# Top-k attention and an MLP mixer: the first five pairs without the adding DMA, another start, orders refitted

## The chip, the cores and the metric

The kernel runs on one core of one Trainium2 chip. The metric is device microseconds (us) of one execution; the time before is a median of 760.9 us over three runs (759.42 to 762.38). A core has a matrix engine (PE, fed by weight loads, PEld), a vector engine (DVE), a scalar engine (ACT), a general engine (POOL), a queue engine that issues transfers (SP), and 16 DMA engines. Each engine works through its own instructions strictly in the order in which they were written down, so a wait of one instruction holds all that stand behind it on that engine.

## The reference

Inputs are q, k and v of 8 batches, 8 heads, 576 rows and 64 columns, in 32 bits, and four weights of a mixer.

```
scores = scale * q @ k^T                      # per batch and head, 576 x 576
kth    = the 32nd largest of each row
scores = where(scores >= kth, scores, -1e9)
attn   = softmax(scores) ; y = attn @ v
x      = y, heads side by side                # per batch 576 x 512
h      = relu(x^T @ w_tok1) @ w_tok2 ; u = x + h^T
out    = u + relu(u @ w_ch1) @ w_ch2
```

## The kernel before

*Pairs, groups and frames.* Two heads make a pair; there are 32 pairs, four to a batch. Of a pair's 2 × 576 score rows the kernel makes five groups (g = 0 to 4): four with 128 rows of each head, and one with the last 64 rows of both. So a pair has nine frames of 128 rows, and the whole work 288.

*The way of a group.* q and k are loaded (L393, L401, L408), turned on PE (`turn`, L426), and kept as qT and kT in SBUF by ACT (L430, L433). PE multiplies them (L488, or L494 for g = 4) into PSUM, ACT copies the scores into a tile Sb (L578). DVE takes the eight largest of each seventh of a row (L588, seven to a row) and from these 56 finds a first threshold in five steps (L593 to L600). POOL negates it (ng, L609) and turns the row's scores into integers that rise above it (L632); ACT counts with Sign how many do (L635); POOL puts eight dummy values, chosen by the count, behind the row (L638); and a last DVE maximum over 584 values (tlo, L643) gives the exact 32nd largest. POOL then makes from it (nt, L651) a mask U, in which what isn't wanted is very low (L666).

*The two ways to the weights.* For most groups (`low` in the code) PE adds the mask in PSUM (L510, L500) and multiplies qT and kT once more on top (L488, L504), and ACT takes the Exp of that into a tile Pm (L676; L682 for g = 4). For the groups listed in `ADDED` ACT takes the Exp straight from Sb, early (L625), into a tile Pe, and POOL issues a DMA that adds the mask U to it in SBUF (L686). In both ways SP then issues a transposing DMA into PT (L690), PE multiplies PT with v (L706), and DVE divides (L715, L716). There are two Pm tiles and four Pe tiles; a tile is free again when its transpose has landed. Before the change one group of every pair but the last is in `ADDED` (g = 1), and in pairs 22 to 30 a second.

*The mixer* of a batch follows its four pairs and is spread over the next ones; its weights come by DMAs that POOL issues at set times in the first 130 us (L336, L346). They are not counted as transfers by the planner.

*The order.* Nothing is ordered by hand. `Plan.add` takes each piece of work with its engine, a planned duration, a due time, what it depends on, and which buffers it takes; `Plan.run` lays them out one after the other: on each engine the piece that can start first, and among those within a few hundredths of a us the one with the least due time. A due time is T × (number of the frame) plus a number for the kind of work from the table `DUE`. So T, `DUE` and the planned durations set the order of all instructions, and nothing else does; real times come out otherwise. `Plan.between` afterwards puts dummy matmuls (`filler`, L368 and L370) into the longer free times that PE has in the plan between 15 and 140 us, to keep its clock up.

*The start.* The first pair has pieces of its own (L446 to L477): k's two heads are issued by ACT and SP; then SP issues the first quarter of q's rows (`some_q(0, 1)`, two transfers), the rest (two) and the last 64 rows (`tail_q`, two, L460), and ACT the last rows of k (L467). PE turns k's first three blocks (k0), q's first quarter (o0), k's last two (k1), and q's other four (o1). Before all this stand the constants: POOL makes an identity (identF), DVE copies it as identB and identN (L313, L314), and then zeroes the last blocks of the q and k tiles (L318), which the loads of those rows have to wait for.

Of the kernel before, what the change touches and what calls it, by code (L numbers as in the profile page):

```python
# [26 lines left out]
ADDED = {(p, 1) for p in range(31)} | {(p, 3) for p in range(22, 31)}  # L27
# [184 lines left out]
def kernel(  # L212
# [98 lines left out]

    make_identity(nc, identF[:, :])
# [4 lines left out]
    for t in qLs + kLs:  # L317
        nc.vector.memset(t[:, 4, :, :], 0.0)  # L318
# [43 lines left out]

    def filler(s, k):
        a = 1024 * s + 1024 - 184

        def f():
            if k is not None:
                nc.tensor.matmul(out=bank[:, a : a + 1], lhsT=identF[:, :], rhs=thi[:, k : k + 1], start=True, stop=True)  # L368
            for _ in range(6):
                nc.tensor.matmul(out=bank[:, a : a + 184], lhsT=identB[:, :], rhs=identF[:, :].bitcast(bf16)[:, 0:184],  # L370
                                 start=True, stop=True)

        return f
# [10 lines left out]
    def pair_ops(p):  # L384
# [51 lines left out]
        if p > 0:  # L436
# [6 lines left out]
            eq = [plan.add("ACT", 0.62, tc_, lambda: keep_q(0, PW), [oq], use=[pq, qT])] * 2  # L443
            ek = [plan.add("ACT", 0.54, tc_ + 0.5 * T, lambda: keep_k(nc.scalar.copy, 0, S), [ok], use=[pk, kT])] * 2
        else:
            def some_q(lo, hi):  # L446
                def f():
                    for h in range(2):
                        nc.sync.dma_start(
                            out=qL.t[:, lo:hi, h, :],  # L450
                            in_=q[b, h0 + h, 0:SM, :].rearrange("(p t) d -> p t d", t=4)[:, lo:hi, :])
                return f
# [24 lines left out]
            eq.append(plan.add("ACT", 0.55, -96.0, lambda: keep_q(P, PW), [o1], use=[pq, qT]))  # L477
# [91 lines left out]
        for g in range(5):  # L569
# [36 lines left out]
        for gs in JOINED if p < END else ((0, 1), (2,), (3,), (4,)):  # L606
            lo, hi = at(frame(gs[-1])[1] + frame(gs[-1])[0] - 1), at(frame(gs[0])[1]) + 1
            nb = Buf("ng")
            o = plan.add("POOL", 0.285, frame(gs[-1])[2] + DUE["ng"], lambda lo=lo, hi=hi, nb=nb: nc.gpsimd.tensor_scalar(  # L609
                out=nb.t[:, 0 : hi - lo], in0=thi[:, lo:hi], scalar1=-1.0, scalar2=None, op0=ALU.mult),  # L610
                         sum((cand[g] for g in gs), []), acq=[nb])
            for g in gs:
                neg[g] = (o, nb, lo)
        for g in range(5):
# [10 lines left out]
            oe = [] if low else [plan.add("ACT", 1.2 if n == 2 else 0.67, t + DUE["ex1"], lambda n=n, Sb=Sb, Pm=Pm: nc.scalar.activation(  # L625
# [4 lines left out]
            for h in range(n):  # L630
# [7 lines left out]
            dm = plan.add("POOL", 0.27, t + DUE["dum"], lambda n=n, i0=i0, X=X: nc.gpsimd.tensor_tensor(  # L638
# [10 lines left out]
        for gs in SETS if p < END else [(g,) for g in range(5) if g not in DIRECT]:  # L649
            nt, lo, hi = Buf("nt"), at(frame(gs[-1])[1] + frame(gs[-1])[0] - 1), at(frame(gs[0])[1]) + 1  # L650
            o = plan.add("POOL", 0.29, frame(gs[-1])[2] + DUE["nt"], lambda lo=lo, hi=hi, nt=nt: nc.gpsimd.tensor_scalar(  # L651
# [4 lines left out]
        for g in range(5):  # L656
# [13 lines left out]
            if low and n == 2:  # L670
                oe = []
                for i in range(2):
                    orr = plan.add("PE", 0.486 if i else 1.18, t + DUE["re"] + 0.01 * i, lambda g=g, i=i, s2=s2, U=U: (
# [11 lines left out]
            else:  # L685
                oe = [plan.add("POOL", 1.08, t + DUE["u"] + 0.02, lambda n=n, U=U, Pm=Pm: nc.gpsimd.dma_start(  # L686
# [45 lines left out]
    def mlp_ops(b):  # L732
# [34 lines left out]
        for cc in range(NC):  # L767
# [23 lines left out]
            ut.append(plan.add("ACT", 0.54, due(0.0) + 1, lambda cc=cc, pb=pb: nc.scalar.copy(  # L791
# [6 lines left out]
        for fc in range(NF):  # L798
# [19 lines left out]
        for s0 in (0, 2, 4) if odd else (0, 2):  # L818
# [4 lines left out]
            for sc in range(s0, s0 + w):  # L823
                for part in range(2):
# [14 lines left out]
                    d = due(1.57 if part else 1.3)  # L839
                    o = plan.add("PE", 1.57 if part else 1.3, d, f, (h2 + wl["c2"] + more) if o is None else [o],  # L840
# [293 lines left out]
    hints = {next(i for i, o in enumerate(order) if o.start > plan.span - d): e for e, d in HINTS.items()}  # L1134
    for i, o in enumerate(order):
# [193 lines left out]
```

## Time and profile before

| | |
|---|---|
| median of three runs | 760.9 us (759.42 to 762.38) |
| the profiled execution | 763.86 us, span 762.1 us |
| busy: PE, DVE, ACT, POOL | 728.7, 718.8, 684.4, 586.4 us |
| DMA | 101.15 MB, 133 GB/s in the mean |

The profile is of one execution, with times from its span's start. The views that the prediction shows are: the busy time of each engine in stretches of the span (with the number of instructions in brackets, the granted clock of PE, and the share of the DMA engines that was busy); the instructions in order of time, with what ended an engine's idle time before one of them in square brackets; the waits, as total, number and longest; the chain of work that ended last, followed back from the end; and groups of like instructions, with their number, busy time and mean duration in ns. A name like "Pm<-bank" is what an instruction writes and reads, L676 a line of the kernel. Matmuls are pipelined and their ends are modelled, so neighbours overlap. A small q behind an engine's name means its queue: an instruction that only issues or waits.

### The profile page before, as it was taken

The page shows a single profiled execution, that of the slowest core. Times are in us where ns is not written, and L with a number is a line of the kernel's source. Part 1 is how long each engine was busy: PE and PEld are TensorE (multiplying, and loading weights), DVE is VectorE, ACT ScalarE, POOL GpSimd, SP SyncE. Part 2 cuts the span into 40 slices and gives each one's busy share as a digit, 9 for nine tenths or more (in the row PEclk, how much of TensorE's full clock was granted, in tenths as well). Part 3 has the DMA queues.
Part 4 walks back from the last instruction along what each step waited for, and adds up shares of the span by engine and source line. Part 5 has one row for each costly group of instructions (what it writes and reads, how often), then busy time and mean ns, then how long its engine had stood idle before and what let it go on. Part 6 is the DMA issues. An engine that isn't in the chain of part 4 may idle for free.

```text
span 762.1 us, 21660 instructions
## 1 busy us (share of the span) xinstructions
PE 728.7 (96%) x6517; PEld 508.1 (67%) x6517; DVE 718.8 (94%) x4466; ACT 684.4 (90%) x1350; POOL 586.4 (77%) x1053
## 2 busy tenths in 40 slices
PE   6989999999999999999999999999989999999997
PEld 4766777677657776667666765667747776677663
DVE  7997999999999999999999999999999999999861
ACT  5868999899889998999989998899989999999852
POOL 3696989987877878778787878877789888988600
PEclk9998999999999999999999999999999999999999
DMA  5598999967887678767787656887759988876602
GB/s 124 91 157 145 142 158 180 170 124 118 148 147 140 125 115 163 151 119 128 118 157 151 121 108 123 168 162 126 139 115 166 152 135 160 137 125 88 123 18 72
DMA packets 293658, 101.15 MB, mean 133 GB/s; under 512 B 269856, under 2 KB 290208, under 8 KB 293536
## 3 DMA queue, kind: packets, MB, share of 16 engines
q1 hardware_dynamic: 279152, 83.86, 59.0%
q0 software_dynamic: 13632, 15.57, 14.6%
q8 instruction: 52, 0.85, 0.4%
q14 instruction: 70, 0.57, 0.2%
q10 hardware_dynamic: 752, 0.30, 0.1%
HBM read 35.85 MB, written 9.44 MB: 59 GB/s over the span
## 4 chain that ended last, share of the span: by engine, by line
DVE 41%; PE 39%; ACT 8%; POOL 6%; issue 3%; DMA 2%; ACTq 0%; DVEq 0%; POOLq 0%; SPq 0%
DVE cd L588 16%; PE bank L488 13%; DVE tlo L643 12%; PE bank L830 4%; PE bank L805 4%; PE bank L706 3%; ACT sign L635 3%; DVE cd L598 3%; PE bank L510 2%; DVE cd L594 2%; POOL U L666 2%; DVE Xb L716 2%; DVE thi L600 2%; PE bank L494 2%; POOL Sb L632 2%
## 5 line engine op out<-in xcount | busy, mean ns | idle before, releaser
L588 DVE MAX8 cd<-Sb 128x8 f32<-128x82 f32 (+1 forms) x2016 | 386.3, 231 | 2.0 <-ACT Sb L578 1.9
L488 PE MATMUL bank<-kT,qT 64*128 64x288 f32 x1712 | 242.2, 422 | 6.2 <-ACT kT L433 3.8
L635 ACT ACTIVATE sign<-Sb,half 128x576 bf16<-128x576 int32 x283 | 226.9, 802 | 20.4 <-POOL Sb L632 12.9
L666 POOL TENSOR_SCALAR U<-Sb,nt 128x576 uint8<-128x576 int32 x283 | 212.3, 750 | 25.7
L632 POOL TENSOR_SCALAR Sb<-Sb,ng 128x576 int32<-128x576 f32 x283 | 217.2, 779 | 13.2 <-ACT Pe L625 6.0
L643 DVE MAX8 tlo<-Sb 128x8 f32<-128x584 uint32 x283 | 214.0, 756 | 8.8 <-POOL Sb L638 8.0
L488 PEld LDWEIGHTS bank<-kT,qT 64*128 64x128 f32 x1712 | 153.9, 188 | 72.7 <-issue 21.7
L578 ACT COPY Sb<-bank 128x576 f32<-128x576 f32 x288 | 167.5, 685 | 10.3 <-PE bank L488 7.5
L676 ACT ACTIVATE Pm<-bank 128x576 bf16<-128x576 f32 x172 | 105.4, 664 | 7.3 <-PE bank L488 7.1
L805 PE MATMUL bank<-UT,wc1b 128*128 128x288 bf16 x672 | 90.2, 286 | 3.6 <-ACT UT L791 1.5
L830 PE MATMUL bank<-wc2b,H 128*128 128x512 bf16 x372 | 88.1, 379 | 0.4 <-ACT H L811 0.4
L805 PEld LDWEIGHTS <-wc1b 128*128 128x128 bf16 x672 | 64.6, 98 | 27.1 <-issue 9.3
L830 PEld LDWEIGHTS <-H 128*128 128x128 bf16 x372 | 34.6, 98 | 40.8 <-issue 6.0
L635 ACT ACTIVATION_READ_ACCUMULATOR sign<-Sb,half 128x1 f32 x283 | 61.7, 218 | 0.0
L651 POOL TENSOR_SCALAR nt<-tlo 128x2 f32<-128x2 f32 (+1 forms) x157 | 35.8, 228 | 32.3 <-DVE tlo L643 12.8
L510 PE MATMUL bank<-U,identN 128*128 128x288 bf16 x344 | 58.1, 288 | 1.2 <-POOL U L666 0.5
L600 DVE MAX8 thi<-cd 128x8 f32<-128x56 f32 x288 | 58.3, 202 | 0.0
L686 POOL DMA_DIRECT2D Pe<-U x40 | 50.4, 1259 | 6.7 <-POOL U L666 4.5
L811 ACT ACTIVATE H<-bank 128x576 bf16<-128x576 f32 x84 | 54.4, 676 | 0.0
L638 POOL TENSOR_TENSOR Sb<-kdum,cnt 128x16 int32<-128x16 int32 (+1 forms) x157 | 36.7, 235 | 21.5 <-ACT sign L635 17.7
L598 DVE MATCH_REPLACE8 cd<-m,cd 128x35 f32<-128x35 f32 x288 | 52.5, 182 | 0.0
L596 DVE MAX8 m<-cd 128x8 f32<-128x35 f32 x288 | 51.9, 180 | 0.1
(140 smaller groups left out, 1067.9 us busy)
## 6 DMA issues: line engine op xcount, KB each, us to landing
Pe<-U POOLq DMA_DIRECT2D x40, 288.0 KB, 4.7
vL<-in_v_dram SPq DMA_DIRECT2D x32, 256.0 KB, 3.0
kL<-in_k_dram SPq DMA_DIRECT2D x63, 128.0 KB, 3.1
qL<-in_q_dram SPq DMA_DIRECT2D x62, 128.0 KB, 2.9
out_dram<-ob SPq DMA_DIRECT2D x15, 512.0 KB, 3.0
wc1b<-in_moe_w_ch_dram POOLq DMA_DIRECT2D x4, 384.0 KB, 5.1
wc2b<-in_moe_w_ch_dram POOLq DMA_DIRECT2D x4, 384.0 KB, 6.5
PT<-Pm SPq DMA_TRANSPOSE x86, 3.9
```

The costliest lines, as they stand in the source:

```text
L488: nc.tensor.matmul(out=halves(s.t)[:, h, :], lhsT=qT.t[rows(h), g * P : (g + 1) * P], rhs=kT.t[rows(h), i * HS : (i + 1) * HS], start=star ...
L578: ev.append(plan.add("ACT", 0.535, t + DUE["cp"] + 0.01 * i, lambda n=n, i=i, s1=s1, Sb=Sb: nc.scalar.copy(out=Sb.t[:, 0:n, i * HS : (i + ...
L588: ss.append(plan.add("DVE", 0.146, t + DUE["seg"] + 1.0 * h, lambda a=a, h=h, cd=cd, Sb=Sb: nc.vector.max(cd.t[:, a, :], Sb.t[:, h, bounds ...
L598: a4 = plan.add("DVE", 0.157, tr_, lambda m8=m8, cd=cd: nc.vector.match_replace(cd.t[:, :, 0:5], m8.t[:, 1, :], cd.t[:, :, 0:5], NEG), [a3 ...
L600: a5 = plan.add("DVE", 0.12, tr_, lambda i=i, cd=cd: nc.vector.max(thi[:, at(i) - 7 : at(i) + 1], cd.t[:, :, :]), [a4] + tops[-1:], use=[cd])
L632: xo.append(plan.add("POOL", 0.725, t + DUE["x"] + 0.9 * h, lambda k=at(i) - lo, h=h, Sb=Sb, X=X, nb=nb: nc.gpsimd.tensor_scalar(out=X.t[: ...
L635: sgn.append(plan.add("ACT", 0.77, t + DUE["sg"] + 0.8 * h, lambda i=i, h=h, X=X: nc.scalar.activation(out=sign[:, :], in_=X.t[:, h, 0:S]. ...
L643: mxs.append(plan.add("DVE", 0.67, t + DUE["mx"] + 1.2 * h, lambda i=i, h=h, X=X: nc.vector.max(tlo[:, at(i) - 7 : at(i) + 1], X.t[:, h, : ...
L666: us.append(plan.add("POOL", 0.84, t + DUE["u"] + 0.01 * h, lambda h=h, k=at(i0 + h) - lo, nt=nt, U=U, X=X: nc.gpsimd.tensor_scalar(out=by ...
L676: oe.append(plan.add("ACT", 0.54, t + DUE["ex"], lambda i=i, s2=s2, Pm=Pm: nc.scalar.activation(out=Pm.t[:, :, i * HS : (i + 1) * HS], in_ ...
L805: nc.tensor.matmul(out=o[:, i, :], lhsT=wc1b[:, cc, fc * P : (fc + 1) * P], rhs=UT.t[:, cc, i * HS : (i + 1) * HS], start=(cc == 0), stop= ...
L830: nc.tensor.matmul(out=po, lhsT=H2.t[:, fc, cs], rhs=wc2b[:, fc, :], start=(fc == 0), stop=False)
```

## The change

1. `ADDED` loses g = 1 of pairs 0 to 4: these five groups go the way of most groups, over Pm.
2. The memsets of the last blocks of the q and k tiles (L318) are moved ahead of the identity.
3. In the first pair q's first quarter is loaded with one transfer for both heads in place of two, and q's last 64 rows are turned and kept by pieces of their own (o2 and a third entry of eq), so that the products of g = 1 to 3 wait for o1 alone.
4. Thirteen dummy matmuls (`warm(3, 13)`) go to the head of PE's work, and three more behind the turning of q's first quarter; the planner counts k's first loads as one us each in place of a half.
5. T, all of `DUE` and some ten planned durations have other values.

```
-ADDED = {(p, 1) for p in range(31)} | {(p, 3) for p in range(22, 31)}
+ADDED = {(p, 1) for p in range(5, 31)} | {(p, 3) for p in range(22, 31)}
...
-T = 1.71610
+T = 1.64060
...
+    for t in qLs + kLs:
+        nc.vector.memset(t[:, 4, :, :], 0.0)
     make_identity(nc, identF[:, :])
...
-    for t in qLs + kLs:
-        nc.vector.memset(t[:, 4, :, :], 0.0)
...
+    def warm(s, n):
+        a = 1024 * s + 1024 - 184
+        for _ in range(n):
+            nc.tensor.matmul(out=bank[:, a : a + 184], lhsT=identB[:, :], rhs=identF[:, :].bitcast(bf16)[:, 0:184],
+                             start=True, stop=True)
...
+            def first_q():
+                nc.sync.dma_start(
+                    out=qL.t[:, 0, :, :],
+                    in_=q[b, h0 : h0 + 2, 0:SM, :].rearrange("h (p t) d -> p t h d", t=4)[:, 0, :, :])
+
+            def more_q():
+                for h in range(2):
+                    nc.sync.dma_start(
+                        out=qL.t[:, 1:4, h, :],
+                        in_=q[b, h0 + h, 0:SM, :].rearrange("(p t) d -> p t d", t=4)[:, 1:4, :])
...
-            la = plan.add("ACT", 0.7, -99.0, main_k(0, nc.scalar), acq=[kL], dma=0.5)
-            lb = plan.add("SP", 0.7, -99.0, main_k(1, nc.sync), [], use=[kL], dma=0.5)
-            q0 = plan.add("SP", 1.3, -98.0, some_q(0, 1), acq=[qL], dma=0.2)
-            q1 = plan.add("SP", 1.3, -97.0, some_q(1, 4), use=[qL], dma=0.7)
+            la = plan.add("ACT", 0.7, -99.0, main_k(0, nc.scalar), acq=[kL], dma=1.0)
+            lb = plan.add("SP", 0.7, -99.0, main_k(1, nc.sync), [], use=[kL], dma=1.0)
+            q0 = plan.add("SP", 0.7, -98.0, first_q, acq=[qL], dma=0.2)
+            q1 = plan.add("SP", 1.3, -97.0, more_q, use=[qL], dma=0.7)
...
-            o0 = plan.add("PE", 0.22, -98.0, turn(pq, qL, (0,)), [q0], acq=[pq, qT], use=[qL])
+            def turn_first():
+                turn(pq, qL, (0,))()
+                warm(3, 3)
+
+            o0 = plan.add("PE", 0.7, -98.0, turn_first, [q0], acq=[pq, qT], use=[qL], lat=-0.3)
             k1 = plan.add("PE", 0.43, -97.0, turn(pk, kL, (3, 4)), [k0, lc], use=[pk, kT, kL])
-            o1 = plan.add("PE", 0.86, -96.0, turn(pq, qL, (1, 2, 3, 4)), [o0, q1, q2], use=[pq, qT, qL])
+            o1 = plan.add("PE", 0.65, -97.5, turn(pq, qL, (1, 2, 3)), [o0, q1], use=[pq, qT, qL])
+            o2 = plan.add("PE", 0.22, -96.0, turn(pq, qL, (4,)), [o1, q2], use=[pq, qT, qL])
...
-            eq.append(plan.add("ACT", 0.55, -96.0, lambda: keep_q(P, PW), [o1], use=[pq, qT]))
+            eq.append(plan.add("ACT", 0.45, -96.5, lambda: keep_q(P, SM), [o1], use=[pq, qT]))
+            eq.append(plan.add("ACT", 0.25, -96.0, lambda: keep_q(SM, PW), [o2], use=[pq, qT]))
...
-                    [eq[g > 0]] + ek[: i + 1 if n == 2 else 2], acq=[s1[i]] + ([Sb] if i == 0 else []), use=[qT, kT, Sb], mode=3 if n == 2 else 0)
+                    [eq[0 if g == 0 else 1 if g < 4 else 2]] + ek[: i + 1 if n == 2 else 2], acq=[s1[i]] + ([Sb] if i == 0 else []), use=[qT, kT, Sb], mode=3 if n == 2 else 0)
...
     hints = {next(i for i, o in enumerate(order) if o.start > plan.span - d): e for e, d in HINTS.items()}
+    warm(3, 13)
     for i, o in enumerate(order):
```

More of the change, by code (lines that the diff above doesn't have):

```diff
@@ L361 @@
             moe_w_ch2[3 * i * P : (3 * i + 3) * P, :].rearrange("(j p) c -> p j c", p=P)))
+    def warm(s, n):
[3 more added lines that the diff above has]
+                             start=True, stop=True)
     def filler(s, k):
-        a = 1024 * s + 1024 - 184
         def f():
             if k is not None:
+                a = 1024 * s + 1024 - 184
                 nc.tensor.matmul(out=bank[:, a : a + 1], lhsT=identF[:, :], rhs=thi[:, k : k + 1], start=True, stop=True)
-            for _ in range(6):
-                nc.tensor.matmul(out=bank[:, a : a + 184], lhsT=identB[:, :], rhs=identF[:, :].bitcast(bf16)[:, 0:184],
-                                 start=True, stop=True)
+            warm(s, 6)
         return f
@@ L442, in pair_ops @@
             tc_ = t0 + DUE["ck"]
-            eq = [plan.add("ACT", 0.62, tc_, lambda: keep_q(0, PW), [oq], use=[pq, qT])] * 2
+            eq = [plan.add("ACT", 0.62, tc_, lambda: keep_q(0, PW), [oq], use=[pq, qT])] * 3
             ek = [plan.add("ACT", 0.54, tc_ + 0.5 * T, lambda: keep_k(nc.scalar.copy, 0, S), [ok], use=[pk, kT])] * 2
         else:
[L446 to L452, printed above, removed]
+            def first_q():
[7 more added lines that the diff above has]
+                        in_=q[b, h0 + h, 0:SM, :].rearrange("(p t) d -> p t d", t=4)[:, 1:4, :])
             def main_k(h, eng):
@@ L608, in pair_ops @@
             nb = Buf("ng")
-            o = plan.add("POOL", 0.285, frame(gs[-1])[2] + DUE["ng"], lambda lo=lo, hi=hi, nb=nb: nc.gpsimd.tensor_scalar(
+            o = plan.add("POOL", 0.23, frame(gs[-1])[2] + DUE["ng"], lambda lo=lo, hi=hi, nb=nb: nc.gpsimd.tensor_scalar(
                 out=nb.t[:, 0 : hi - lo], in0=thi[:, lo:hi], scalar1=-1.0, scalar2=None, op0=ALU.mult),
@@ L634, in pair_ops @@
                     op0=ALU.add, op1=ALU.mult), [no] + oe, use=[Sb, nb]))
-                sgn.append(plan.add("ACT", 0.77, t + DUE["sg"] + 0.8 * h, lambda i=i, h=h, X=X: nc.scalar.activation(
+                sgn.append(plan.add("ACT", 0.72, t + DUE["sg"] + 0.8 * h, lambda i=i, h=h, X=X: nc.scalar.activation(
                     out=sign[:, :], in_=X.t[:, h, 0:S].bitcast(i32), func=AF.Sign, bias=half[:, :],
                     accum_out=cnt[:, i : i + 1]), [xo[h]], use=[X], lat=0.7))
-            dm = plan.add("POOL", 0.27, t + DUE["dum"], lambda n=n, i0=i0, X=X: nc.gpsimd.tensor_tensor(
+            dm = plan.add("POOL", 0.22, t + DUE["dum"], lambda n=n, i0=i0, X=X: nc.gpsimd.tensor_tensor(
                 out=X.t[:, 0:n, S:XW].bitcast(i32), in0=kdum[:, :].unsqueeze(1).to_broadcast([P, n, NDUM]),
@@ L685, in pair_ops @@
             else:
-                oe = [plan.add("POOL", 1.08, t + DUE["u"] + 0.02, lambda n=n, U=U, Pm=Pm: nc.gpsimd.dma_start(
+                oe = [plan.add("POOL", 0.95, t + DUE["u"] + 0.02, lambda n=n, U=U, Pm=Pm: nc.gpsimd.dma_start(
                     out=Pm.t[:, 0:n, 0:S].bitcast(u16), in_=U.t[:, 0:n, :], accum_op=ALU.add), us, use=[U, Pm], lat=4.1, dma=1.02 * n)]
@@ L790, in mlp_ops @@
             o = plan.add("PE", 0.98, due(0.98), f, [h1] + wl["w2"], acq=[pb] + ([UT] if cc == 0 else []), use=[X, H1, pb])
-            ut.append(plan.add("ACT", 0.54, due(0.0) + 1, lambda cc=cc, pb=pb: nc.scalar.copy(
+            ut.append(plan.add("ACT", 0.58, due(0.0) + 1, lambda cc=cc, pb=pb: nc.scalar.copy(
                 out=UT.t[:, cc, 0:S].rearrange("p (a b) -> p a b", a=2), in_=halves(pb.t)), [o],
@@ L838, in mlp_ops @@
                     more = ([tails["h2"]] + ut[NC:]) if s0 == 4 else []
-                    d = due(1.57 if part else 1.3)
-                    o = plan.add("PE", 1.57 if part else 1.3, d, f, (h2 + wl["c2"] + more) if o is None else [o],
+                    d = due(1.57 if part else 1.14)
+                    o = plan.add("PE", 1.57 if part else 1.14, d, f, (h2 + wl["c2"] + more) if o is None else [o],
                                  acq=[pb, ob] if o is None else [], use=[pb, H2] + ([UT] if part else []))
```

18 lines of the change are left out of this document (9 added, 9 removed).

## Prediction, made before the changed kernel was run

> **What bounds the kernel now.** I read the busy times first, then the stretches: where each engine is busy, and where the vector engine (DVE) is not.
>
> ```profile
> PE 728.7 (96%) x6517; PEld 508.1 (67%) x6517; DVE 718.8 (94%) x4466; ACT 684.4 (90%) x1350; POOL 586.4 (77%) x1053
> ```
>
> ```profile
> core 0: us, PE busy (x) PEld busy (x) DVE busy (x) ACT busy (x) POOL busy (x), PEclk, DMA share, GB/s
> 9.00:60.00 51.00, 43.53 (x368) 33.87 (x369) 50.66 (x365) 37.07 (x72) 33.93 (x63) 0.98 0.77 125
> 60.00:70.00 10.00, 10.00 (x98) 6.70 (x98) 4.89 (x27) 8.03 (x17) 5.35 (x9) 0.77 0.91 139
> 70.00:712.00 642.00, 627.30 (x5630) 436.94 (x5628) 633.94 (x3990) 612.26 (x1215) 535.73 (x966) 1.00 0.78 138
> 712.00:762.00 50.00, 43.40 (x413) 28.13 (x410) 24.90 (x59) 24.71 (x44) 7.08 (x8) 0.99 0.31 74
> ```
>
> From 9 to 712 us DVE is busy for 689.5 of 703 us, and the change gives it no less to do. So only four things can be won: a start before 9 us, the 5.1 us idle at 60 to 70, the 8.1 us spread over 70 to 712, and something of the last 50 us, which are a chain through PE. The hole at 60 to 70 is the only large one; the waits and the order of time of that stretch follow it back.
>
> ```profile
> DVE tlo L643 <- POOL Sb L638: 4.6, 1, 4.6
> PE bank L368 <- ACT qT L430: 3.9, 1, 3.9
> ACT Pm L682 <- DMA PT<-Pm: 2.7, 1, 2.7
> ```
>
> ```profile
> 40.73 1.27 POOL L686 DMA_DIRECT2D Pe<-U  x1
> ...
> 45.50 1.19 ACT L676 ACTIVATE Pm<-bank 128x576 bf16<-128x576 f32 x2 [2.01 <-PE bank L488]
> ...
> 47.27 1.35 SPq L690 DMA_TRANSPOSE PT<-Pe  x1
> ...
> 48.72 2.68 SPq L690 DMA_TRANSPOSE PT<-Pm  x1
> ...
> 48.84 0.77 POOL L346 DMA_DIRECT2D ob<-in_moe_w_tok_dram  x1
> ...
> 56.78 0.65 ACT L682 ACTIVATE Pm<-bank 128x576 bf16<-128x576 f32 x1 [2.65 <-DMA PT<-Pm]
> ...
> 59.53 4.21 PE L488 MATMUL bank<-kT,qT 64*128 64x288 f32 x16
> 63.68 1.10 PE L510 MATMUL bank<-U,identN 128*128 128x288 bf16 x4
> 64.71 2.21 PE L488 MATMUL bank<-kT,qT 64*128 64x288 f32 x16
> ...
> 66.49 0.77 DVE L643 MAX8 tlo<-Sb 128x8 f32<-128x584 uint32 x1 [4.62 <-POOL Sb L638]
> ...
> 68.66 0.22 DVE L715 RECIPROCAL rds<-bank 128x10 f32<-128x10 f32 x1 [0.45 <-PE bank L706]
> ```
>
> ```profile
> 48.72 7.98 DMA PT<-Pm
> ```
>
> Read it backwards. DVE stood 4.62 and 0.45 us (5.07 in all). PE behind it had first stood 3.9 us, then run cold: the same sixteen products took 4.21 us and, once the clock was back, 2.21. PE stood because ACT stood 2.65 us, in order, at L682, which needs one of the two Pm slots; that slot was still being read by the transpose issued at 48.72, which took 7.98 us to land. That Pm had been ready at 46.69 (45.50 + 1.19). It was issued 2.03 us later because SP issues in order and ahead of it stood the transpose of Pe, which waits for the adding DMA of 40.73 to land. I call all this the hold.
>
> **The first five pairs without the adding DMA.** Five groups of pairs 0 to 4 go the way the others go.
>
> ```profile
> L488 PE MATMUL bank<-kT,qT 64*128 64x288 f32 x312 | 46.4, 435 | 1.9 <-ACT kT L433 1.4 <-ACT Sb L578 0.5
> L370 PE MATMUL bank<-identF,identB 128*128 128x184 bf16 x324 | 30.4, 244 | 1.7 <-ACT Pm L676 0.9 <-ACT kT L433 0.7
> L676 ACT ACTIVATE Pm<-bank 128x576 bf16<-128x576 f32 x30 | 18.4, 654 | 2.1 <-PE bank L488 2.0
> L510 PE MATMUL bank<-U,identN 128*128 128x288 bf16 x60 | 10.9, 295 | 0.9 <-POOL U L666 0.5 <-ACT Pm L682 0.3
> L625 ACT ACTIVATE Pe<-Sb 128x1152 bf16<-128x1152 f32 x7 | 8.2, 1173 | 0.0
> L686 POOL DMA_DIRECT2D Pe<-U x5 | 6.3, 1265 | 0.9 <-POOL U L666 0.6 <-POOL nt L651 0.2
> ```
>
> These groups are the stretch from 15 to 140 us. POOL loses 5 × 1.265 = 6.3 us and the DMA engines five transfers of 288 KB. ACT swaps one 1.17 us Exp for a pair of evictions (1.19 us by the x2 row above): nothing. PE gains per group 4 of L510 (10.9/60 × 4 = 0.73) and 8 of L488 (46.4/312 × 8 = 1.19), together 1.92, so 9.6 us over five. This is hidden by the dummy matmuls of L370, 30.4 us in the same stretch, which the planner puts only into free time of PE; without that cover it would cost the 9.6 us, since PE is the neighbour that fills Sb.
>
> What it does to the hold: no transpose waits for an adding DMA any more, so the transposes behind it go out up to 2.03 us earlier and the slot is free by as much. Of ACT's 2.65 us 0.6 stay. PE then stands some 1.9 instead of 3.9 us and, I assume, keeps its clock: L488 falls by 2.00 (4.21 - 2.21), and L510's first four by about 0.4 (1.10 against 4 × 0.18). 2.03 + 2.00 + 0.4 = 4.4 of 5.07. Bounds: nothing (the transpose at 48.72 met the weight load issued at 48.84, and that stays) and all 5.07. I take -4.4, as the wait in the Pm row starts with the late issue. POOL's 1.26 us, gone from each of four more pairs, meets 8.06 us of DVE idle over 70 to 712; I take -0.5 for it, bounds 0 and -1.5.
>
> The Trainium skill, page "DMA: Bandwidth & Descriptors", section "Issuing engines are not separate DMA queues", says that transfers of all issuing engines run on the same 16 DMA engines and interleave. By that rule the whole 7.98 us is crowding, the late issue is worth little, and the hold term would lie nearer to 0 than to -4.4; the landing of 7.98 us right beside the weight load agrees with it.
>
> **The start.**
>
> ```profile
> 1.33 1.51 DVE L313 CAST identB<-identF 128x128 bf16<-128x128 f32 x1 [1.33 <-POOL identF masks.py:199]
> ...
> 1.48 2.32 SPq L449 DMA_DIRECT2D qL<-in_q_dram  x4
> ...
> 2.88 0.30 DVE L318 MEMSET qL<- 128x128 f32 x2
> ...
> 3.36 0.65 ACTq L467 DMA_DIRECT2D kL<-in_k_dram  x1
> ...
> 3.85 0.87 PE L426 MATMUL bank<-identF,kL 128*128 128x128 f32 x3 [3.85 <-DMA kL<-in_k_dram]
> ...
> 6.18 0.47 PE L426 MATMUL bank<-identF,kL 128*128 128x128 f32 x1 [0.33 <-DMA kL<-in_k_dram]
> ...
> 7.96 0.64 ACT L578 COPY Sb<-bank 128x576 f32<-128x576 f32 x1 [2.35 <-PE bank L488]
> ...
> 8.63 0.68 DVE L588 MAX8 cd<-Sb 128x8 f32<-128x82 f32 x4 [1.59 <-ACT Sb L578]
> 8.80 1.11 PE L426 MATMUL bank<-identF,qL 128*128 128x128 f32 x4
> ```
>
> ```profile
> 6.58 2.29 PE L488 MATMUL bank<-kT,qT 64*128 64x288 f32 x8
> ...
> 10.60 1.73 PE L488 MATMUL bank<-kT,qT 64*128 64x288 f32 x12 [0.69 <-ACT qT L430]
> ```
>
> ```profile
> 58.66 0.94 PE bank L370 x6
> ```
>
> Before, the tail of k is issued at 3.36, after the memsets of qL and kL, and its transpose at 6.18 is the last thing ahead of the first products. With the memsets first (four, about 0.6 us, while DVE waits for identF anyway) it goes out near 1.4, behind the ACT queue's first load, and lands two us earlier. SP issues three transfers instead of four for q's main rows (2.32/4 = 0.58 saved), so the tails of q come 0.6 us earlier. Nothing of that wait is left. What is late next is PE. Thirteen dummy matmuls now stand at the head of its queue and need identB, ready at 2.84 (1.33 + 1.51); at 0.94/6 = 0.157 each, cold, they end at 4.9, one us after k's main rows have landed (3.85). Behind them, by the due numbers in the code: k's three transposes (0.28 each by the 8.80 row, so to 5.7), q's first and three dummies (to 6.5), and then, which is new, q's other three (due -97.5, ahead of k's last two at -97), k's two, q's tail: six at 0.28, to 8.2. Only then the first four products: 1.15 us (half of 2.29), copy 0.64 plus hand-over: DVE starts at about 10.0 instead of 8.63, +1.4. With the clock up from about 6.5 four products cost 0.58 (1.73/12 × 4), half, and so I halve the six, 0.14 each: to 7.9, DVE at 8.6; no loss. If instead the planner puts the products ahead of q's rows, 0.8 us less, at 7.8. So -0.8 to +1.4. The rows show PE cold for 5 us and more after its first matmul (3.85 to the 8.80 row) and again after the restart at 58 (fast from 64.7), but both times with pauses or half-filled arrays; here it works without a pause. I take +0.5.
>
> By the Trainium skill, page "TensorE: Matmul & The Clock Gate", section "Part 1: The HAM clock gate", about 3.4 us of sustained work raise the clock. By that rule it would be up at 6.3 and the start term 0; by the rows above, cold until 9, it would be +1.4.
>
> **The refitted orders.** T, the due numbers and some planned durations change, so each engine gets the same instructions in another order over the whole run. No row gives their price. Bounds: they can win about half of the 8.06 us of DVE idle over 70 to 712, -4, and lose as much, +4; with both ends alike I take 0.
>
> **Sum.** -4.4 - 0.5 + 0.5 + 0 = -4.4. The profiled execution took 763.86 us (span 762.1 and 1.76 around it): 759.5. It lies 2.96 above the median of the runs shown (760.9, from 759.42 to 762.38), so against that median the forecast is 756.5, between 753.5 and 759.5 by the start's and the refit's smaller misses.
>
> **Rivals.** *The hold stays.* The transpose that was late ran beside a weight load which the planner doesn't count as a transfer and which comes at the same time again. For it: 7.98 us of landing against a few for the issue. Against it: two us of late issue go for certain. Then -0.5 + 0.5 and a little: 761.
>
> *Slower: two Pm slots for five groups.* The adding groups had slots of their own (Pe); now all five groups of a pair turn through the two Pm slots. In pair 0 a slot was held from 45.50 to about 56.7, 11.2 us; five at that rate on two slots are 28 us, and DVE needs 718.8/32 = 22.5 us a pair. So ACT would stand at L676 or L682, in order, with the copies into Sb behind it: 28 - 22.5 = 5.5 us on top of the old hold, in pair 0 alone, as a Pm lands in 3.6 us in the median:
>
> ```profile
> DMA to landing us min/median/max: 2.6/3.6/8.0
> ```
>
> With +0.5 at the start: 766.9. It decides once a slot is held for over 9 us (22.5 × 2 / 5). Against it: part of those 11.2 us was the wait behind Pe.
>
> *The refit wins too.* If the new orders also close half of DVE's small gaps: 756.5 - 4 = 752.5. For it: 8 us are there. Against it: each is under a us, and PE is busy for 627 of the same 642 us.
>
> **How the numbers follow.** Forecast 0.42, hold stays 0.20, Pm slots 0.16, refit wins too 0.22. A measurement of this kernel tells no change from one of about 0.5%, 3.8 us: faster means under 757.1. Faster: 0.30 of the forecast's 0.42 and 0.22 give 0.52. Within: 0.12 of the forecast, 0.18 of the hold, 0.01 gives 0.31. Slower: 0.15 of the slots and 0.02 of the hold, 0.17. The range, 750 to 766, holds the forecast, the hold, nearly all of the refit and half of the slots.
>
> **What would show it.** Right: L686 falls from 40 to 35, L676 rises from 172 to 182; no DVE wait over 2 us between 20 and 130; no wait of ACT for PT<-Pm over 1 us. Start: first L588 between 8 and 10 us, the products cold or warm telling which. Wrong: an ACT wait at L676 or L682 as long as before, a granted clock under 1.00 after 15 us, or DVE idle over 70 to 712 far from 8.

## The result, and the profile after

The changed kernel takes 771.18 us in the median (four runs, 769.97 to 772.27), the kernel before 760.51 (four, 759.42 to 762.38): a ratio of 1.0134 [1.011, 1.0158]. It is slower by 10.7 us, outside the range of the forecast. Its profiled execution took 769.97 us, with a span of 768.2. Two executions lie far outside the rest, one of the kernel with the five groups alone (1864.98 us) and one of the kernel before beside it (1853.38), and are left out of the medians below.

The busy times of each engine in four stretches, first before, then after. Columns: stretch, its length, then busy time and number of instructions of each engine, the granted clock, the DMA share, GB/s.

```profile
core 0: us, PE busy (x) PEld busy (x) DVE busy (x) ACT busy (x) POOL busy (x), PEclk, DMA share, GB/s
0.00:10.00 10.00, 5.38 (x18) 2.94 (x18) 5.14 (x36) 2.88 (x5) 4.28 (x10) 1.00 0.49 118
10.00:70.00 60.00, 52.62 (x460) 40.05 (x462) 54.82 (x385) 44.50 (x88) 39.27 (x71) 0.94 0.80 128
70.00:700.00 630.00, 615.30 (x5542) 430.14 (x5541) 622.47 (x3943) 600.63 (x1191) 525.30 (x944) 1.00 0.78 139
700.00:762.10 62.10, 55.40 (x503) 34.92 (x499) 36.37 (x107) 36.35 (x69) 17.51 (x30) 0.99 0.38 77
```

```profile
0.00:10.00 10.00, 7.11 (x42) 5.97 (x44) 4.36 (x32) 3.37 (x6) 4.29 (x10) 1.00 0.51 118
10.00:70.00 60.00, 54.94 (x485) 40.87 (x482) 58.86 (x395) 51.30 (x106) 44.62 (x84) 1.00 0.87 145
70.00:700.00 630.00, 607.73 (x5387) 420.79 (x5414) 609.21 (x3857) 587.70 (x1165) 504.21 (x910) 1.00 0.74 133
700.00:768.20 68.20, 60.28 (x575) 39.12 (x580) 47.45 (x188) 43.01 (x82) 26.93 (x45) 0.99 0.41 87
```

Take DVE's busy time from each stretch. Its idle time goes from 4.9 to 5.6 us at the start, from 5.2 to 1.1 at 10 to 70 (the hold is gone, and the clock there is 1.00), from 7.5 to 20.8 at 70 to 700, and from 25.7 to 20.8 after that. DVE's own work grows by 1.1 (718.8 to 719.9). So 0.8 - 4.0 + 13.3 - 5.0 + 1.1 = 6.1, the difference of the two spans. The loss is in the long middle; some of it comes back at the end, as work that was pushed there (188 DVE instructions after 700 us in place of 107). Without the 4.0 of the hold the sum is 10.2, about the difference of the medians: more on this below.

What DVE waits for in the middle, as waits over 70 to 700 us (total us, number, longest), before and then after; and the page's row of the last maximum, in the same order:

```profile
POOL Sb L638 <- ACT sign L635: 12.3, 18, 1.6
POOL nt L651 <- DVE tlo L643: 11.7, 15, 1.7
...
DVE tlo L643 <- POOL Sb L638: 3.1, 8, 0.9
```

```profile
POOL nt L663 <- DVE tlo L655: 32.5, 32, 1.9
POOL Sb L650 <- ACT sign L647: 15.5, 26, 2.7
DVE tlo L655 <- POOL Sb L650: 12.9, 27, 1.7
```

```profile
L643 DVE MAX8 tlo<-Sb 128x8 f32<-128x584 uint32 x283 | 214.0, 756 | 8.8 <-POOL Sb L638 8.0
```

```profile
L655 DVE MAX8 tlo<-Sb 128x8 f32<-128x584 uint32 x283 | 214.4, 758 | 15.1 <-POOL Sb L650 13.9
```

The instructions are the same, 283 with a mean of 756 and 758 ns; their wait is not. It is no new hole. There are 27 waits in place of 8, none over 1.7 us. They lie in a circle: DVE waits for POOL's dummies, POOL for ACT's count, and POOL, in order, for DVE's result (32.5 us in place of 11.7). One turn of it, after, in order of time:

```profile
122.01 0.80 ACT L647 ACTIVATE sign<-Sb,half 128x576 bf16<-128x576 int32 x1
122.69 0.21 ACT L647 ACTIVATION_READ_ACCUMULATOR sign<-Sb,half 128x1 f32 x1
122.99 0.77 ACT L647 ACTIVATE sign<-Sb,half 128x576 bf16<-128x576 int32 x1
123.67 0.19 ACT L647 ACTIVATION_READ_ACCUMULATOR sign<-Sb,half 128x1 f32 x1
123.94 0.21 POOL L650 TENSOR_TENSOR Sb<-kdum,cnt 128x16 int32<-128x16 int32 x1 [1.00 <-ACT sign L647]
124.19 0.77 DVE L655 MAX8 tlo<-Sb 128x8 f32<-128x584 uint32 x1 [1.02 <-POOL Sb L650]
```

The two counts of a group start 0.98 us apart. The changed plan allows 0.72 for one.

The start, after, in order of time:

```profile
1.10 0.31 DVE L313 MEMSET kL<- 128x128 f32 x2
1.44 0.66 ACTq L473 DMA_DIRECT2D kL<-in_k_dram  x1
2.89 2.17 PE L366 MATMUL bank<-identF,identB 128*128 128x184 bf16 x13 [2.89 <-DVE identB L315]
4.86 0.85 PE L429 MATMUL bank<-identF,kL 128*128 128x128 f32 x3
6.29 0.90 PE L429 MATMUL bank<-identF,qL 128*128 128x128 f32 x3
6.98 0.63 PE L429 MATMUL bank<-identF,kL 128*128 128x128 f32 x2
7.41 0.42 PE L429 MATMUL bank<-identF,qL 128*128 128x128 f32 x1
7.76 1.15 PE L500 MATMUL bank<-kT,qT 64*128 64x288 f32 x4
9.63 0.68 DVE L600 MAX8 cd<-Sb 128x8 f32<-128x82 f32 x4 [1.62 <-ACT Sb L590]
```

The memsets and the tail of k come early, as written; but six turnings of q and k (6.29 to 7.76) stand ahead of the first products, these run cold, at about half speed (1.15 us for four, where 0.58 was reckoned with the clock up), and DVE's first maximum is at 9.63 in place of 8.63. The two counts of instructions that the prediction names as signs, 35 and 182, are there too:

```profile
L698 POOL DMA_DIRECT2D Pe<-U x35 | 43.8, 1253 | 6.8 <-POOL U L678 5.7
```

```profile
L688 ACT ACTIVATE Pm<-bank 128x576 bf16<-128x576 f32 x182 | 113.0, 662 | 8.8 <-PE bank L500 8.8
```

### The profile page after: what moved, and what is told of

Same layout as the page of the kernel before. It is cut to its first block, busy times and chain, and to the rows that moved or that the text cites. A ratio compares the mean times of both kernels' runs of the same rounds, so it can differ in the third digit from the quotient of the medians.

```text
span 768.2 us, 21614 instructions
## 1 busy us (share of the span) xinstructions
PE 730.1 (95%) x6480; PEld 506.7 (66%) x6515; DVE 719.9 (94%) x4466; ACT 685.4 (89%) x1356; POOL 580.1 (76%) x1048
## 3 DMA queue, kind: packets, MB, share of 16 engines
q0 software_dynamic: 12272, 14.09, 13.1%
## 4 chain that ended last, share of the span: by engine, by line
PE 43%; DVE 26%; POOL 12%; ACT 11%; issue 6%; DMA 1%; ACTq 0%; DVEq 0%; POOLq 0%
PE bank L500 13%; DVE cd L600 9%; DVE tlo L655 9%; PE bank L817 6%; POOL U L678 4%; POOL Sb L644 4%; ACT sign L647 4%; PE bank L842 4%; ACT Sb L590 3%; PE bank L522 3%; PE bank L718 3%; PE bank L516 2%; PE bank L429 2%; PE bank L506 2%; ACT Pm L688 2%
## 5 line engine op out<-in xcount | busy, mean ns | idle before, releaser
L500 PE MATMUL bank<-kT,qT 64*128 64x288 f32 x1752 | 246.5, 421 | 4.1 <-ACT kT L436 3.2
L678 POOL TENSOR_SCALAR U<-Sb,nt 128x576 uint8<-128x576 int32 x283 | 212.0, 749 | 25.7
L644 POOL TENSOR_SCALAR Sb<-Sb,ng 128x576 int32<-128x576 f32 x283 | 207.9, 750 | 7.4 <-ACT Pe L637 0.6
L590 ACT COPY Sb<-bank 128x576 f32<-128x576 f32 x288 | 169.3, 672 | 4.7 <-PE bank L500 1.9
L688 ACT ACTIVATE Pm<-bank 128x576 bf16<-128x576 f32 x182 | 113.0, 662 | 8.8 <-PE bank L500 8.8
L842 PE MATMUL bank<-wc2b,H 128*128 128x512 bf16 x347 | 86.3, 379 | 1.5 <-issue 0.2
L663 POOL TENSOR_SCALAR nt<-tlo 128x2 f32<-128x2 f32 (+1 forms) x157 | 33.3, 213 | 53.6 <-DVE tlo L655 32.9
L522 PE MATMUL bank<-U,identN 128*128 128x288 bf16 x364 | 62.5, 288 | 3.8 <-POOL U L678 2.5
L647 ACT ACTIVATION_READ_ACCUMULATOR sign<-Sb,half 128x1 f32 x283 | 59.5, 210 | 0.0
L650 POOL TENSOR_TENSOR Sb<-kdum,cnt 128x16 int32<-128x16 int32 (+1 forms) x157 | 36.6, 235 | 25.7 <-ACT sign L647 19.4
L698 POOL DMA_DIRECT2D Pe<-U x35 | 43.8, 1253 | 6.8 <-POOL U L678 5.7
```

The costliest lines, as they stand in the source:

```text
L500: nc.tensor.matmul(out=halves(s.t)[:, h, :], lhsT=qT.t[rows(h), g * P : (g + 1) * P], rhs=kT.t[rows(h), i * HS : (i + 1) * HS], start=star ...
L522: nc.tensor.matmul(out=halves(s.t)[:, h, :], lhsT=identN[:, :], rhs=U.t[:, h, i * HS : (i + 1) * HS], start=True, stop=False)
L590: ev.append(plan.add("ACT", 0.535, t + DUE["cp"] + 0.01 * i, lambda n=n, i=i, s1=s1, Sb=Sb: nc.scalar.copy(out=Sb.t[:, 0:n, i * HS : (i + ...
L644: xo.append(plan.add("POOL", 0.725, t + DUE["x"] + 0.9 * h, lambda k=at(i) - lo, h=h, Sb=Sb, X=X, nb=nb: nc.gpsimd.tensor_scalar(out=X.t[: ...
L647: sgn.append(plan.add("ACT", 0.72, t + DUE["sg"] + 0.8 * h, lambda i=i, h=h, X=X: nc.scalar.activation(out=sign[:, :], in_=X.t[:, h, 0:S]. ...
L678: us.append(plan.add("POOL", 0.84, t + DUE["u"] + 0.01 * h, lambda h=h, k=at(i0 + h) - lo, nt=nt, U=U, X=X: nc.gpsimd.tensor_scalar(out=by ...
```

## The experiments

Each was timed against the kernel before on the same chip, whose medians there were 760.5 to 761.9. All but two keep what is computed; the two with half a count say so. "The orders" are T, `DUE` and the ten planned durations that the change sets; together they decide the order of every engine's instructions.

### The parts of the change: edits alone, orders alone, durations or due numbers alone

First the edits, with T, `DUE` and the durations of before:

```
-T = 1.64060
+T = 1.71610
...
-    ck=-21.800, cp=-192.710, dum=-170.670, ex=-117.230, ex1=37.887, lq=7.360, m6=-103.130, mlp=5.847,
+    ck=-24.678, cp=-144.260, dum=-172.040, ex=-64.742, ex1=38.952, lq=3.203, m6=-41.460, mlp=15.068,
...
-                sgn.append(plan.add("ACT", 0.72, t + DUE["sg"] + 0.8 * h, lambda i=i, h=h, X=X: nc.scalar.activation(
+                sgn.append(plan.add("ACT", 0.77, t + DUE["sg"] + 0.8 * h, lambda i=i, h=h, X=X: nc.scalar.activation(
```

> All edits of the change, but T, the due numbers and the ten planned durations of the kernel before. Theory 'orders' (the refitted numbers are what loses; the edits themselves win the hold and lose one us at the start): 756 to 760, with DVE idle over 70 to 712 near the 8 us of before. Theory 'edits' (five more groups through the two Pm slots and the dummies at PE's head lose): 768 to 772. Theory 'any order that was not searched for this program loses' (every new order leaves small waits): 764 to 772, with small DVE waits spread over the whole run.

Measured: 766.93, 1.0073 [1.0047, 1.0098]. Then the reverse, the kernel before with nothing but the new T, `DUE` and durations:

> The kernel before with the new T, due numbers and ten durations, and none of the edits. 'Orders': 768 to 775, DVE idle spread in pieces under 2 us. 'Edits': 759 to 763. 'Any order not searched for': 764 to 775.

Measured: 773.99, 1.0173 [1.0138, 1.0208]. The orders alone lose more than the whole change does. Where they lose it is the same place (windows and waits over 70 to 700 us, orders alone):

```profile
70.00:700.00 630.00, 607.46 (x5404) 423.12 (x5402) 610.24 (x3857) 593.02 (x1170) 515.40 (x922) 0.99 0.75 137
```

```profile
POOL nt L651 <- DVE tlo L643: 25.5, 27, 1.8
...
POOL Sb L638 <- ACT sign L635: 15.8, 20, 1.9
DVE tlo L643 <- POOL Sb L638: 14.8, 24, 1.6
```

DVE is idle for 19.8 us there, and its wait for the dummies is 14.8, close to after's 20.8 and 12.9, without any edit of the work.

Next, one half of the orders at a time: the changed kernel with the old durations, and the changed kernel with the old T and `DUE`.

> The changed kernel with the ten planned durations of before; T and due numbers stay new. If it is the shortened durations (POOL's small pieces 0.22 in place of 0.27 to 0.29, Sign 0.72 in place of 0.77) that make the plan put DVE's last maximum ahead of what it waits for, the idle time of DVE ahead of that maximum falls from 15 us to under 10 and the time to 762 to 766. If it is the due numbers: 770 or more.

> The changed kernel with T and the due numbers of before; the ten durations stay new. If the due numbers lose: 758 to 763. If the shortened durations lose: 768 to 773.

Measured: 775.19, 1.0183 [1.0157, 1.0208], and 776.74, 1.0213 [1.018, 1.0245]. Both halves by themselves are worse than both together, so neither half alone is the culprit, and the parts don't add: edits +6.0, orders +13.1, both 10.7.

### The smallest steps, and an order changed for no reason

The memsets moved, every other instruction in the old order; and this with the thirteen dummies at the head of PE:

```
+    for t in qLs + kLs:
+        nc.vector.memset(t[:, 4, :, :], 0.0)
     make_identity(nc, identF[:, :])
...
-    for t in qLs + kLs:
-        nc.vector.memset(t[:, 4, :, :], 0.0)
...
+    warm(3, 13)
```

> The kernel before, with only the four memsets of the q and k tiles moved ahead of the identity; the order on every engine is otherwise the same, instruction by instruction. The tail of k should be issued near 1.4 us and the first products stand at 5.9 instead of 6.58: first maximum of DVE near 7.9 instead of 8.63, and the time 0.5 to 0.8 us less (760.2), if DVE carries its lead to the end; 760.9 if the hold at 57 to 66 us swallows it.

> The same, with thirteen dummy matmuls at the head of PE besides, and the order otherwise as before. If they cost what they did in the changed kernel, k's first transposes start near 4.8 instead of 3.85 and the first maximum of DVE is at 8.5 to 8.9, some 0.5 to 1 us after the kernel with the memsets alone; if the clock they raise pays for them, at 8.0 or earlier.

Measured: 760.13, 0.9997 [0.9979, 1.0015], and 761.13, 1.0009 [0.9991, 1.0027]. The starts, memsets alone and then with the dummies:

```profile
1.44 0.66 ACTq L467 DMA_DIRECT2D kL<-in_k_dram  x1
4.01 0.87 PE L426 MATMUL bank<-identF,kL 128*128 128x128 f32 x3 [4.01 <-DMA kL<-in_k_dram]
6.16 2.29 PE L488 MATMUL bank<-kT,qT 64*128 64x288 f32 x8
8.21 0.68 DVE L588 MAX8 cd<-Sb 128x8 f32<-128x82 f32 x4 [1.58 <-ACT Sb L578]
```

```profile
4.87 0.84 PE L432 MATMUL bank<-identF,kL 128*128 128x128 f32 x3
6.81 1.27 PE L494 MATMUL bank<-kT,qT 64*128 64x288 f32 x8
8.29 0.83 DVE L594 MAX8 cd<-Sb 128x8 f32<-128x82 f32 x5 [1.01 <-ACT Sb L584]
```

Memsets first bring the first maximum from 8.63 to 8.21. The dummies hold k's turning back by 0.9 us (4.01 to 4.87) and win it back on warm products (2.29 to 1.27 for eight): 8.29. Neither is seen in the total. In the changed kernel it is 9.63: the products start at 7.76 in place of 6.81, behind the turnings put ahead of them, and their first four are slow again.

The five groups alone (`ADDED` as in the change, nothing else), and the kernel before with every entry of `DUE` moved at random by at most 0.5, no work changed:

```
-ADDED = {(p, 1) for p in range(31)} | {(p, 3) for p in range(22, 31)}
+ADDED = {(p, 1) for p in range(5, 31)} | {(p, 3) for p in range(22, 31)}
```

```
-    ck=-24.678, cp=-144.260, dum=-172.040, ex=-64.742, ex1=38.952, lq=3.203, m6=-41.460, mlp=15.068,
+    ck=-24.222, cp=-143.812, dum=-172.483, ex=-65.157, ex1=39.287, lq=3.439, m6=-41.290, mlp=14.876,
```

> The kernel before with only the five groups taken out of ADDED; T, due numbers and durations of before. The planner's own span for it is 748.9 us, for the kernel before 742.4. Theory 'the plan under the old durations tells the order's worth' (chip time is that span plus some 18 us, as in the kernel before, the edits with old orders and the old durations): 766 to 768.5, and no hold. 'The edit is free and wins the hold': 755 to 758. 'Two Pm slots are too few': ACT waits for the landing of PT over 3 us in the first 130 us.

> The kernel before with each due number moved by a random amount of at most 0.5, nothing else; over half of the neighbours in the orders of ACT, DVE and POOL change by it. The planner's own span rises from 742.4 to 752.4. 'The plan under the old durations tells the order's worth': 769 to 772. 'Due numbers matter little': 759 to 763.

Measured: 770.09, 1.0119 [1.0089, 1.0149], and 768.47, 1.0101 [1.0082, 1.0119]. The random shift is the key run. It changes which instruction follows which for 72% of DVE's neighbouring pairs (ACT 63%, POOL 69%, PE 46%) and costs 7.7 us with the same work and the same durations. So a part of the change can't be priced by making that part alone and planning anew: the run measures a new order together with the part. That holds for the five groups alone, and for the edits alone.

### Other fits of the same edits

Here T and `DUE` were searched anew for a short plan, with the old durations: twice for the five groups and the memsets, once for all edits. Of the first fit, T and the first line of `DUE`:

```
-T = 1.71610
+T = 1.70150
...
-    ck=-24.678, cp=-144.260, dum=-172.040, ex=-64.742, ex1=38.952, lq=3.203, m6=-41.460, mlp=15.068,
+    ck=-36.166, cp=-326.586, dum=-104.075, ex=-133.807, ex1=44.112, lq=-19.984, m6=-111.288, mlp=15.387,
```

> The kernel before with the five groups out of ADDED and the memsets first; the ten planned durations of before; T and due numbers fitted anew so that the planner's own span under these durations falls from 748.9 to 737.1. 'The plan under the old durations tells the order's worth' (span plus 16 to 22): 753 to 759, faster than before. 'The plan is no guide to the chip, only a hand-picked order is good': 764 to 772. 'Five groups through two Pm slots lose by themselves': over 764 with ACT waiting for PT.

> The same kernel with another fit of T and due numbers, of a planner's span of 738.5. By the plan under the old durations: 754.5 to 760.5; if only a hand-picked order is good: 764 to 772.

> All edits of the change (dummies at PE's head and the parted loads of the first pair too), the ten durations of before, T and due numbers fitted to a planner's span of 740.9. By the plan under the old durations: 757 to 763, at least 8 us under the changed kernel (771.2), whose span under its own shortened durations was 735.2. If the plan is no guide: 768 or more.

Measured: 760.71, 0.9976 [0.9955, 0.9998]; 765.31, 1.0053 [1.003, 1.0077]; 766.96, 1.007 [1.0035, 1.0105]. The first two have the same work and differ by 4.6 us, in the order alone. So there is an order in which the five groups cost nothing. In the second fit most of the loss is one stall before 70 us, which begins with ACT's wait of 4.4 us for a Pm slot (shown further down); that wait is the second rival of the prediction. The first is the only new order below the kernel before, with an interval that ends at 0.9998; as one of several fits it is not claimed as a better version.

### The counts: shorter in truth, longer in the plan

Counts over half of each row, in the changed kernel and in the kernel before, each in its own order:

```
-                    out=sign[:, :], in_=X.t[:, h, 0:S].bitcast(i32), func=AF.Sign, bias=half[:, :],
+                    out=sign[:, 0:HS], in_=X.t[:, h, 0:HS].bitcast(i32), func=AF.Sign, bias=half[:, :],
...
-    with tc.If(wrong > 0, label="exact"):
+    with tc.If(wrong > 37000, label="exact"):
```

> The changed kernel, with the Sign of ACT over half a row only (288 of 576 values: the count is wrong, so the last maxima and the output are not the reference's; the jump to the exact path is shut). The orders on all engines stay the same, instruction by instruction. If the changed orders lose because they count on a Sign of 0.72 us where the chip takes 0.96 from one to the next, the DVE idle time ahead of the last maxima (15 us) falls under 5 and the time by 10 us or more, to 758 to 762. If they lose elsewhere (PE or POOL), it falls by no more than the kernel before does under the same cut.

> The kernel before under the same cut (Sign over half a row, exact path shut, orders the same). Its own DVE idle ahead of the last maxima is some 4 to 8 us: it should win 2 to 6 us, to 755 to 759. The difference between the two gains is what the changed orders lose to late counts.

Measured: 758.35, 0.9973 [0.9956, 0.9989], and 755.93, 0.9934 [0.9913, 0.9955]. The same relief of ACT wins 12.8 us in the new order (from 771.18, measured at another time, where before took 760.51) and 5.1 in the old (from 760.99). The difference of the two kernels shrinks from 10.7 to 2.4 us. So some 8 us of the loss are waits that ACT's time makes. Stretch 70 to 700, first the changed kernel, then the kernel before, with half counts; and the changed kernel's wait over the same stretch:

```profile
70.00:700.00 630.00, 612.18 (x5477) 426.65 (x5506) 616.64 (x3903) 550.08 (x1184) 512.16 (x927) 1.00 0.74 135
```

```profile
70.00:700.00 630.00, 616.49 (x5544) 433.27 (x5571) 624.15 (x3951) 552.55 (x1201) 528.25 (x952) 1.00 0.78 139
```

```profile
DVE tlo L655 <- POOL Sb L650: 9.8, 21, 0.8
```

DVE's idle time falls from 20.8 to 13.4 in the one and from 7.5 to 5.9 in the other. But the wait for the dummies falls only from 12.9 to 9.8: the shorter count does not take that wait away, and the rest of the gain comes from other waits. The count itself is not the whole of the circle.

If the plan's short count (0.72 where the chip takes 0.98 from one to the next) made the fit choose such orders, a longer one should help. The kernel of the five groups and the memsets, planned with a longer count, in two fits:

```
-                sgn.append(plan.add("ACT", 0.77, t + DUE["sg"] + 0.8 * h, lambda i=i, h=h, X=X: nc.scalar.activation(
+                sgn.append(plan.add("ACT", 0.86, t + DUE["sg"] + 0.8 * h, lambda i=i, h=h, X=X: nc.scalar.activation(
```

> The kernel before with the five groups out of ADDED and the memsets first; planned durations of before but for Sign, 0.86 in place of 0.77 (the chip takes 0.77 ahead of other work and 0.96 from one Sign to the next); T and due numbers fitted to this plan (planner's span 746.4). If late counts are what a plan with a short Sign hides, these orders hold up better on the chip: 10 to 15 us over the span, 756 to 761, under the same program fitted with Sign at 0.77 (760.7 and 765.3, middle 763). If the length of Sign in the plan doesn't matter: 762 to 767.

> The same with another fit (span 746.7). Late counts: 756 to 761. Otherwise: 762 to 767.

Measured: 765.7, 1.0056 [1.0037, 1.0075], and 769.74, 1.0129 [1.0102, 1.0155]: no gain in time. But these two lose in another place. Both have a stall at 50 to 70 us in which ACT waits for a Pm slot, 3.5 us in the first and 10.6 in the second, while DVE's idle time in the middle is 10.4 and 7.5: about as in the other fits, and in the second as in the kernel before. So a longer count makes no better order as a whole; that the shortened durations did no harm is not shown by this.

### All of them side by side

The end of the plan is what the kernel's own planner works out from its planned durations. DVE's idle time is from each kernel's one profiled execution, worked out as above.

| kernel | end of the plan | chip, median | DVE idle 10-70 | 70-700 | 700 to end |
|---|---|---|---|---|---|
| before | 742.4 | 760.5 | 5.2 | 7.5 | 25.7 |
| memsets first, same order | 742.4 | 760.1 | 0.3 | 8.0 | 25.3 |
| memsets and dummies, same order | 742.4 | 761.1 | 2.7 | 7.8 | 25.6 |
| five groups, new fit 1 | 737.1 | 760.7 | 1.7 | 9.3 | 24.9 |
| five groups, new fit 2 | 738.5 | 765.3 | 7.2 | 9.7 | 23.4 |
| longer count planned, fit 1 | 746.4 | 765.7 | 6.8 | 10.4 | 25.0 |
| edits, old orders | 749.9 | 766.9 | 0.7 | 16.5 | 24.2 |
| all edits, new fit | 740.9 | 767.0 | 4.5 | 12.5 | 26.9 |
| due numbers at random | 752.4 | 768.5 | 0.5 | 13.4 | 30.5 |
| longer count planned, fit 2 | 746.7 | 769.7 | 8.7 | 7.5 | 29.5 |
| five groups alone | 748.9 | 770.1 | 3.3 | 17.5 | 24.3 |
| after | 735.2 | 771.2 | 1.1 | 20.8 | 20.8 |
| orders alone | 736.0 | 774.0 | 1.0 | 19.8 | 24.0 |
| after, old durations | 756.9 | 775.2 | 0.1 | 22.6 | 27.1 |
| after, old T and due numbers | 738.5 | 776.7 | 2.2 | 18.9 | 27.5 |

For the orders that were not fitted to their own plan, the plan was a fair guide. With the 18.1 us by which the kernel before ends later on the chip than in its plan, it gives 768.0 for the edits with old orders (measured 766.9), 775.0 for the old durations (775.2), 767.0 for the five groups alone (770.1) and 770.5 for the random due numbers (768.5). The three fits with old durations were to reach 755 to 759 by the same sum and took 760.7 to 767.0. This would fit a search that gains most where the plan is wrong; no run shows it.

The changed kernel has the shortest plan of all and the fourth longest time. The three orders that were planned with the short durations end 36.0 to 38.2 us later on the chip than in the plan, the kernel before 18.1, and the new fits with old durations 23.6 to 26.8. Nor is the loss always in the middle: the random due numbers lose 4.8 us at the end (30.5 in place of 25.7), and the second fit with the longer count, with 7.5 us in the middle, loses at both ends.

What the shortened durations hide can be worked out with the kernel's own planner; this is arithmetic on the plan and no run. Keep the order and the buffers of the changed kernel as they are, and put in the ten durations of before: its plan then ends at 755.5 in place of 735.2. The orders alone end at 756.1 in place of 736.0, and the changed kernel with the old T and due numbers at 758.0 in place of 738.5. These are 13.1, 13.7 and 15.6 us behind the 742.4 of the kernel before, and on the chip they lost 10.7, 13.1 and 15.8. Put back one at a time in the changed kernel, the count (0.72 to 0.77) moves the end by 10.1 us and nt (0.22 to 0.29) by 6.3, more than any other of the ten: both stand in the circle above. The longer figures are not the truer ones for each piece (nt takes 0.23 us in the trace of before and 0.21 in that of after). That they left room in the orders is an inference.

## Why the prediction was wrong

*The refitted orders: the step that failed.* The prediction gave them ±4 us, as "about half of the 8.06 us of DVE idle over 70 to 712, -4, and lose as much, +4". The idle time that is there bounds what an order can win by closing it. It does not bound what another can lose. The orders alone cost 13.1 us, and DVE's idle time in the middle went from 7.5 to 19.8. Even a meaningless reordering cost 7.7. The term should have been a loss with a wide bound: of the twelve other orders in the table, the changed kernel's among them, eleven are slower than that of before. The prediction's own sign for being wrong, DVE idle over 70 to 712 "far from 8", is what came.

*The hold: right in the profile, wrong against the median.* In the changed kernel DVE is busy for 58.86 of the 60 us from 10 to 70, the clock there is 1.00, and its trace shows no wait of ACT for a Pm slot. These rows of the view of PT tell who waited for the transposes, before and then after; the 0.4 us that stay are a weight load of PE at L718, which needs PT itself:

```profile
  ACT Pm L682: 3.0, 2
```

```profile
  PEld L718: 0.4, 1
```

That is what the forecast said. But the gain was taken off a time that hadn't paid it. The profiled execution of before had a mean granted clock of 0.995 and 763.86 us. Of 68 timed executions of that kernel, beside all these runs, 3 had 0.995 (mean 765.3 us), 2 had 0.996 (762.7), 30 had 0.997 (761.8), and 33 had 0.998 to 1.000 (760.0); their median is 761.1. They have no trace, so what they had of the hold is inferred from the clock. Two traces bear on it, both with every order of before kept, the adding DMA of the first pairs included. With the memsets moved (mean clock 0.998) there is no hold: DVE, third busy time of this row, works 9.75 of the 10 us. With the dummies besides (0.997) there is a smaller one, in which ACT waits 1.6 us for a Pm slot and DVE works 7.46:

```profile
60.00:70.00 10.00, 8.35 (x108) 6.23 (x104) 9.75 (x59) 9.70 (x22) 9.27 (x18) 1.00 1.08 178
```

```profile
60.00:70.00 10.00, 9.22 (x108) 6.41 (x105) 7.46 (x44) 9.63 (x22) 7.46 (x15) 0.94 1.18 182
```

So, by the clock, -4.4 belonged to the few executions like the profiled one. Against the median the term was between 0 and about -1 us, an estimate from the 761.1 of all and the 760.0 of those with the highest clock. Nor is the adding DMA shown as its cause. The orders alone and the random due numbers keep it and have no hold (DVE idle 1.0 and 0.5 us from 10 to 70). The two fits with the longer count, without it, have a hold of the same kind, and so has the second fit of the five groups (waits from 40 to 70 us):

```profile
POOL Sb L638 <- ACT sign L635: 6.6, 3, 3.5
DVE tlo L643 <- POOL Sb L638: 6.5, 2, 3.6
...
ACT Pm L676 <- DMA PT<-Pm: 4.4, 1, 4.4
```

That a transpose is late there with no adding DMA ahead of it fits the crowding that the prediction took from the Trainium skill, page "DMA: Bandwidth & Descriptors", section "Issuing engines are not separate DMA queues"; no run here separates crowding from late issue.

*The start: order right, price a little low.* The order on PE was read exactly (k's three, q's first and dummies, q's three, k's two, q's tail, products). The first maximum is 1.0 us late, forecast +0.5 within -0.8 to +1.4. The choice to halve the price between cold and warm was the miss: the first four products ran cold, 1.15 us, as in the upper bound.

*POOL's relief, -0.5.* POOL's work fell from 586.4 to 580.1 us, by the 6.3 forecast. Its gain can't be seen beside the orders; the best fit of the five groups measures 0.9976, with an interval of -3.4 to -0.2 us. That holds -0.5 us, but its order is another too.

*Two Pm slots* were not the reason: the changed kernel has no wait of ACT for them. The rival is real in other orders, though: 4.4 us in the second fit of the five groups, 3.5 and 10.6 in the two with the longer count. Whether the old way over Pe would have spared these orders the wait was not tried.

*The forecast's sum* was thus -4.4 - 0.5 + 0.5 + 0. Measured against the median it is 0 to -1 for the hold, +0.8 to +1.0 for the start and some 10 to 11 for the orders, a remainder, since the parts don't add. Shown is that the orders lose by themselves (13.1 us with the same work), and where: in many waits on the circle of DVE, POOL and ACT, of which some 8 us go when ACT has less to do. Why the search chose them is argued: the durations with which it planned were shorter, and with those of before the plan itself puts these orders 13 to 16 us behind. Open stay what each duration does by itself on the chip, and why the fits with old durations also end later than planned.

## What to carry to other kernels

Where a planner writes the order, a changed piece of work and a changed order are two changes: time a random shift of the due numbers first (the one tried here cost 1.0%), and believe no part's price that is smaller than that. Idle time in a profile bounds what a new order may win, never what it may lose, and a shorter plan made with shorter planned durations says nothing until the new order is timed with the old durations too (here 755.5 in place of 735.2, against 742.4). Before taking a large stall off the median, compare the profiled execution's time and mean clock with the timed ones: it may be a stall of a few executions only.

## What the runs showed of the hardware that was not expected

In these two traces PE did not become fast at one fixed time after it began to work. The same thirteen dummies start at 2.89 us in the changed kernel and at 2.90 in the one with memsets and dummies. In the latter the products are fast from their first on, at 6.81 (eight in 1.27 us), so the rise came at most 3.9 us after the dummies' start. In the changed kernel the four at 7.76, 4.9 us after it, are still slow (0.29 us each), and the first fast ones are these, 5.9 us after it (0.15 each):

```profile
8.74 0.89 PE L500 MATMUL bank<-kT,qT 64*128 64x288 f32 x6
```

The granted clock of the stretch 0 to 10 us is given as 1.00 all the same, so there the speed is read from durations. The Trainium skill, page "TensorE: Matmul & The Clock Gate", section "Part 1: The HAM clock gate", gives about 3.4 us of sustained work before the rise, and says that the moment varies by 500 ns either way from run to run. The trace with memsets and dummies agrees with that (at most 3.9); the changed kernel lies above it by 1.5 to 2.5 us, with turnings and no pause between dummies and products. With one trace of each kernel it is not shown what the difference comes from.
